# The last batch of an attention and expert kernel set up like the other three

## The chip, the cores and the metric

The kernel runs on one core of a Trainium2 chip. The metric is the device time of one execution in microseconds; the time before is the median of three runs.

## What is computed

Four batches of 11,456 tokens of width 128 pass through an attention over 49 agents, and its output through a layer of eight experts of which each token uses one. Cut to what matters:

```python
def sm(a, b):                       # softmax of scale * a @ b^T
    ...
agent_v = sm(agents, k) @ v         # 49 x 128 for each batch
x = sm(q, agents) @ agent_v         # the token
...
expert_idx = argmax(normalized(x) @ normalized(expert_emb).T / tau)
for e in range(8):
    h = np.maximum(x[mask] @ w1[e], 0.0)        # 1024 hidden units
    out[mask] = gate_w[mask, None] * (h @ w2[e])
```

## The kernel before

**Approach.** The tokens of a batch are mixtures of the same 49 vectors, and nearly all of them choose the same expert. `pick_expert` (L556) picks that expert for the batch, loads its weights, and ranks its 1024 hidden units by how safely their sign is the same for every token. The least safe `NMS[b] * 128` are the *layer units*: they are computed in full with their Relu. The next `FVS[b]` are the *checked units*: they are taken as linear, and a test on every token shows whether their sign held. The rest are linear by a bound. All linear units are folded into one 49 x 128 matrix, `lin`. Before, batches 0 to 2 have 256 layer units (`NMS` 2) and 320 checked units, the last batch 384 (`NMS` 3) and 512.

**Tiles.** A batch has 23 tiles (`NT`): 22 of 512 tokens and one of 192. For each tile and each group of 128 layer units `ffn_mm1` (L1032) makes two 512-wide matmuls (L1040, L1041), a Relu on ScalarE (L1044) and a residual on VectorE (L1045); `ffn_mm2` (L1048) makes twelve 128-wide ones (L1068 to L1070), and once per tile eight for `lin` (L1059). `ffn_out` (L1072) applies the gate on VectorE (L1083) and issues the output DMA on ScalarE's queue (L1089).

**Queries and checks.** A query unit (`q_unit`, L759) is up to 8 columns of 128 tokens, two tiles' worth: a load and a transposing DMA on SP, transposes, scores, exponentials and routing sums; `route_group` (L837) makes gates. Its result `tt` lies in one of eight buffers (`TB`), which is given back when the unit's layers and checks are through. `proved` (L910) makes the check for one column: one matmul with `vm` (L918), then a reduction on VectorE (L923, three columns in eight) or a summed Relu on ScalarE (L921).

**Failed tokens.** When a batch's 90 columns are checked, `mark_strays` (L933) marks the failed tokens. In batches 0 to 2 it keeps up to 3 of a partition and 128 in all that belong to the batch's expert, and spawns `fix` (L1182): the rows are gathered by an indirect DMA on POOL, the expert's weights are loaded again, `answer` (L1118) computes attention and expert in full for these 128 rows (L1121 to L1178), and an indirect DMA on POOL (L1179) overwrites their rows of the output. Other marked tokens are left to `stray` (L1198), which redoes one group per call. One call, `stray_first` (L1273), is emitted in the last batch's stage, after `fix` of batch 2. The rest is done in a loop behind everything, whose count is known only at run time (L1475 to L1483).

**Order.** The program is emitted in ticks, four to a tile, so 92 to a batch. Generators (`spawn`) are resumed at tick or half-tick intervals, and each `yield` is a step of them. A scheduler then places the instructions on each engine in a simulated order, in which emission order is a priority and the layers' first matmuls are drawn ahead; SP keeps the emitted order. `plan` (L1359) says when loads and queries are due; the keys and values of batch b run in the stage of batch b - 1. `prove()` is called once per tick, or twice if 12 or more checks are waiting (L1467). A write to `out` waits for the writes to `out` emitted before it.

Of the kernel before, what the change touches and what calls it, by code (L numbers as in the profile page):

```python
# [29 lines left out]
def kernel(ctx: ExitStack, tc: tile.TileContext, q, k, v, agents, emb, tau, w1, w2, out):  # L30
# [6 lines left out]
    NF = F // P  # L37
    NMS = [2] * (B - 1) + [3]
    FVS = [P * 5 // 2] * (B - 1) + [4 * P]
    FW = 4 * P  # L40
# [892 lines left out]
    def mark_strays(b):  # L933
# [32 lines left out]
        yield 1  # L966
        if b < B - 1:
            cand = sm.tile([P, NCOL], F32, name="mine", tag="mine", bufs=1)
# [103 lines left out]
    def ffn_out(b, t):  # L1072
# [14 lines left out]
        else:  # L1087
            dst = ob[P * J :, :].rearrange("(p j) d -> p j d", j=REM_J)
        act.dma_start(out=dst, in_=o[:p, :n])  # L1089


# [25 lines left out]

    def answer(xq, ix, gt, aT, avn, w1s, w2s):  # L1118

# [52 lines left out]
        for f in range(NF):  # L1172
            pe.matmul(out=t_[:, :D], lhsT=h[:, f, :], rhs=w2s[:, f, :], start=(f == 0), stop=(f == NF - 1))
            if f % 2 == 1:
                yield 1
        ring[hs][1] = now[0]
        o = sm.tile([P, D], F32, name="so", tag="so", bufs=1)
        dve.tensor_scalar(o, t_[:, :D], gt, None, ALU.mult)  # L1178
        pool.indirect_dma_start(out=out, out_offset=bass.IndirectOffsetOnAxis(ap=ix, axis=0), in_=o, in_offset=None,  # L1179
                                bounds_check=B * N - 1, oob_is_err=False)  # L1180

    def fix(b):  # L1182

        bt = batches[b]
        while not (hasattr(batches[b + 1], "vm") and (b == 0 or hasattr(batches[b - 1], "fixed"))):
            yield 1
        none = sm.tile([P, 1], F32, name="none", tag="none", bufs=1)
        ix = sm.tile([P, 1], I32, name="ix", tag="ix")
        dve.tensor_scalar(none, bt.fix[:, :1], 0.5, 2 * BIG, ALU.is_lt, ALU.mult)
        yield 1  # L1190
        dve.scalar_tensor_tensor(out=ix, in0=bt.fix[:, :1], scalar=-1.0, in1=none, op0=ALU.add, op1=ALU.add)
        w1s, w2s = load_expert(bt.e0i)
        xq = gather(ix)
        yield 14
        yield from answer(xq, ix, bt.fix[:, 1:], aT_all[:, b], av_all[:, b], w1s, w2s)
        bt.fixed = True
# [76 lines left out]
    def stray_first():  # L1273
# [7 lines left out]
        yield 1  # L1281
        dve.tensor_scalar(it, cums[-1][:, NG - 1 :], 1.0, None, ALU.min)


# [71 lines left out]

    QD = 6

    def plan():  # L1359
# [9 lines left out]
        for b in range(B):  # L1369
            for u in range(NU):  # L1370
                if b > 0 or u >= LEAD:
                    qs.append((at + QD, "q", b, u))
                    at += UT * TICKS if u < NU - 1 else TICKS
        return sorted(kv), qs
# [70 lines left out]
    with tc.manual_schedule(engines={mybir.EngineType.SP}):  # L1445
        due = []
        for i in range(len(ticks) + LAG):
# [14 lines left out]
            while due and due[0][0] <= i:  # L1462
# [3 lines left out]
                step2(b, t, f)  # L1466
            for _ in range(1 if len(jobs) < 12 else 2):  # L1467
                prove()
# [44 lines left out]
```

## Time and profile before

| | |
|---|---|
| median of 3 runs | 800.2 us (796.48 to 808.74) |
| profiled execution | 793.86 us, its span 792.1 us |
| busy share of the span | PE 90%, PEld 76%, DVE 78%, ACT 61%, POOL 44% |
| granted TensorE clock, mean | 0.958 |
| the chain that ended last, by engine | PE 56%, DVE 22%, DMA 11%, ACT 6% |

PE are TensorE's matmuls, PEld its weight loads, which overlap them; DVE is VectorE, ACT ScalarE, POOL GpSimd, SP the engine that issues most loads. Times are microseconds from the start of the span, unless marked ns. A matmul is shown for as long as it is under way, so neighbours overlap, and the step from start to start is its price on a full engine. The granted clock is a share of full speed.

### The profile page before, as it was taken

The page shows a single profiled execution, that of the slowest core. Times are in us where ns is not written, and L with a number is a line of the kernel's source. Part 1 is how long each engine was busy: PE and PEld are TensorE (multiplying, and loading weights), DVE is VectorE, ACT ScalarE, POOL GpSimd, SP SyncE. Part 2 cuts the span into 40 slices and gives each one's busy share as a digit, 9 for nine tenths or more (in the row PEclk, how much of TensorE's full clock was granted, in tenths as well). Part 3 has the DMA queues.
Part 4 walks back from the last instruction along what each step waited for, and adds up shares of the span by engine and source line. Part 5 has one row for each costly group of instructions (what it writes and reads, how often), then busy time and mean ns, then how long its engine had stood idle before and what let it go on. Part 6 is the DMA issues. An engine that isn't in the chain of part 4 may idle for free.

```text
span 792.1 us, 21166 instructions
## 1 busy us (share of the span) xinstructions
PE 715.1 (90%) x8161; PEld 602.9 (76%) x8161; DVE 616.4 (78%) x1639; ACT 485.5 (61%) x1229; POOL 345.1 (44%) x602
## 2 busy tenths in 40 slices
PE   8976789989997989899999699999998898999995
PEld 6976678977786768778888488778886686787774
DVE  5554998877674998966788898966789888698876
ACT  2334656866665765666767853766579346667762
POOL 5000453246413744645524633684537336254510
PEclk9987799999996999989999999999999999999997
DMA  8756029978627957955787528975342334333211
GB/s 329 205 191 249 28 28 283 272 171 227 190 89 201 260 131 167 226 151 144 220 210 196 116 78 207 252 194 172 108 130 74 89 102 126 92 87 94 84 41 47
DMA packets 164049, 124.01 MB, mean 157 GB/s; under 512 B 84967, under 2 KB 140347, under 8 KB 163947
## 3 DMA queue, kind: packets, MB, share of 16 engines
q1 hardware_dynamic: 150571, 99.02, 48.1%
q10 hardware_dynamic: 13120, 23.47, 8.6%
q8 instruction: 65, 1.06, 0.6%
q14 instruction: 37, 0.30, 0.1%
q0 software_dynamic: 256, 0.15, 0.1%
HBM read 79.14 MB, written 23.72 MB: 130 GB/s over the span
## 4 chain that ended last, share of the span: by engine, by line
PE 56%; DVE 22%; DMA 11%; ACT 6%; issue 4%; POOL 1%; SPq 0%; ACTq 0%; POOLq 0%; DVEq 0%
PE sp L773 6%; PE fTp L390 5%; PE avp L487 5%; PE sp L411 5%; PE vp L918 5%; PE yp L1068 4%; PE hp L1040 3%; PE yp L1069 3%; PE yp L1070 3%; DMA tt<-e 3%; PE hp L1041 3%; DVE hl L1045 3%; PE yp L1059 3%; DMA kt<-in_k_dram 2%; DVE ot L1083 2%
## 5 line engine op out<-in xcount | busy, mean ns | idle before, releaser
L1045 DVE SCALAR_TENSOR_TENSOR hl<-hp,hh 128x512 f16<-128x512 f32 (+1 forms) x207 | 136.9, 665 | 30.3 <-ACT hh L1044 29.8
L1068 PE MATMUL yp<-w2p,hh 128*128 128x128 f16 (+1 forms) x810 | 156.7, 222 | 0.8 <-ACT hh L1044 0.4
L1069 PE MATMUL yp<-w2p,hh 128*128 128x128 f16 (+1 forms) x810 | 156.4, 222 | 0.0
L1070 PE MATMUL yp<-w2p,hl 128*128 128x128 f16 (+1 forms) x810 | 152.5, 222 | 3.4 <-DVE hl L1045 3.4
L921 ACT ACTIVATE vp<-vp,la 128x320 f32<-128x320 f32 (+1 forms) x224 | 121.4, 542 | 53.2 <-PE vp L918 39.4
L1044 ACT ACTIVATE hh<-hp 128x512 f16<-128x512 f32 (+1 forms) x207 | 120.5, 587 | 52.1 <-PE hp L1041 44.4
L918 PE MATMUL vp<-vm,tt 128*128 128x320 f16 (+1 forms) x360 | 108.5, 320 | 8.1 <-DVE hl L1045 2.9
L1068 PEld LDWEIGHTS <-hh 128*128 128x128 f16 (+1 forms) x810 | 81.5, 101 | 18.5 <-ACT hh L1044 4.2
L1070 PEld LDWEIGHTS <-hl 128*128 128x128 f16 (+1 forms) x810 | 81.0, 100 | 18.2 <-issue 3.9
L773 PEld LDWEIGHTS sp<-aT_all,fT 128*128 128x128 f32 x720 | 86.6, 192 | 4.3 <-ACT gh L683 0.6
L773 PE MATMUL sp<-aT_all,fT 128*128 128x49 f32 x720 | 87.6, 271 | 0.6 <-ACT gh L683 0.4
L1069 PEld LDWEIGHTS <-hh 128*128 128x128 f16 (+1 forms) x810 | 81.2, 100 | 7.1 <-issue 0.7
L923 DVE TENSOR_REDUCE vmin<-vp 128x1 f32<-128x320 f32 (+3 forms) x136 | 72.1, 531 | 18.3 <-PE vp L918 18.2
L1040 PE MATMUL hp<-tt,gh 128*128 128x512 f16 (+1 forms) x207 | 77.5, 377 | 7.3 <-ACT vp L921 2.2
L1041 PE MATMUL hp<-tt,gl 128*128 128x512 f16 (+1 forms) x207 | 77.4, 376 | 0.0
L788 POOL TENSOR_TENSOR e<-qe,e 128x392 f16<-128x392 f32 (+1 forms) x44 | 37.8, 860 | 79.9 <-ACT e L787 74.4
L869 POOL TENSOR_TENSOR nrm<-qq,half 128x16 f32<-128x16 f32 (+2 forms) x28 | 69.2, 2472 | 0.3
L1083 DVE TENSOR_TENSOR ot<-yp,gs 128x512 f32<-128x512 f32 (+1 forms) x92 | 61.4, 668 | 8.4 <-PE yp L1070 8.1
L395 ACT COPY fT<-fTp 128x512 f32<-128x512 f32 (+1 forms) x78 | 43.7, 563 | 36.4 <-PE fTp L390 28.2
L1059 PE MATMUL yp<-lin,tt 128*128 128x128 f16 x720 | 64.2, 220 | 1.2 <-DVE ot L1083 1.1
L390 PE MATMUL fTp<-ident,qt 128*128 128x128 f32 x360 | 59.4, 301 | 5.8 <-DVE hl L1045 2.4
L393 DVE COPY fT<-fTp 128x512 f32<-128x512 f32 x70 | 47.7, 682 | 18.1 <-PE fTp L390 16.7
(358 smaller groups left out, 1735.4 us busy)
## 6 DMA issues: line engine op xcount, KB each, us to landing
kt<-in_k_dram SPq DMA_DIRECT2D x44, 512.0 KB, 6.8
vt<-in_v_dram SPq DMA_DIRECT2D x44, 512.0 KB, 5.0
qt<-in_q_dram SPq DMA_DIRECT2D x44, 512.0 KB, 5.4
out_dram<-ot ACTq DMA_DIRECT2D x88, 256.0 KB, 2.9
w1s<-in_moe_w_dram SPq DMA_DIRECT2D x8, 512.0 KB, 3.7
w2s<-in_moe_w_dram SPq DMA_DIRECT2D x8, 512.0 KB, 5.8
tt<-e SPq DMA_TRANSPOSE x44, 3.5
kt<-in_k_dram SPq DMA_DIRECT2D x4, 96.0 KB, 3.0
```

The costliest lines, as they stand in the source:

```text
L390: pe.transpose(out=tp[:, c * p : (c + 1) * p], in_=src[:p, c0 + c, :], identity=ident[:p, :p])
L773: pe.matmul(out=s[:p, c * A : (c + 1) * A], lhsT=xT[:, c * p : (c + 1) * p], rhs=aT_all[:, b, :], start=True, stop=True)
L918: pe.matmul(out=z[:p, :FV], lhsT=tts[b, u][:, c * p : (c + 1) * p], rhs=bt.vm, start=True, stop=True)
L921: act.activation(z[:p, :FV], z[:p, :FV], AF.Relu, bias=bt.l[:p, at], scale=-1.0, accum_out=bt.vsum[:p, at])
L1040: pe.matmul(out=hp[:, :m], lhsT=bt.gh[:, fs], rhs=tt, start=True, stop=False)
L1041: pe.matmul(out=hp[:, :m], lhsT=bt.gl[:, fs], rhs=tt, start=False, stop=True)
L1044: h_last[:] = [act.activation(hh[:, :m], hp[:, :m], AF.Relu)]
L1045: dve.scalar_tensor_tensor(out=hl[:, :m], in0=hp[:, :m], scalar=0.0, in1=hh[:, :m], op0=ALU.max, op1=ALU.subtract)
L1059: pe.matmul(out=yp[:p, c, :], lhsT=tc_, rhs=bt.lin[:, h], start=(c == 0 and h == 0), stop=False, skip_group_check=True)
L1068: pe.matmul(out=y, lhsT=hh[:, cs], rhs=wh, start=False, stop=False, skip_group_check=True)
L1069: pe.matmul(out=y, lhsT=hh[:, cs], rhs=wl, start=False, stop=False, skip_group_check=True)
L1070: y_last[:] = [pe.matmul(out=y, lhsT=hl[:, cs], rhs=wh, start=False, stop=last, skip_group_check=True)]
```

## The change

All four batches get 256 layer units and 320 checked units. `mark_strays` runs its candidate part, and spawns `fix`, for the last batch too. `fix` of the last batch starts once `stray_first` has appended to `strayed`; and before its scatter it waits until all 23 output DMAs of its batch are emitted (`last.outs < NT`). In `plan` the queries of the last batch are due at 0.6 of the distance (`RUN`): 4.8 ticks instead of 8 from unit to unit. In the last batch's ticks `prove()` is always called twice.

```diff
-    NMS = [2] * (B - 1) + [3]
-    FVS = [P * 5 // 2] * (B - 1) + [4 * P]
+    NMS = [2] * B
+    FVS = [P * 5 // 2] * B
...
-        if b < B - 1:
+        if True:
             cand = sm.tile([P, NCOL], F32, name="mine", tag="mine", bufs=1)
...
         act.dma_start(out=dst, in_=o[:p, :n])
+        batches[b].outs = getattr(batches[b], "outs", 0) + 1
...
-    def answer(xq, ix, gt, aT, avn, w1s, w2s):
+    strayed = []
+
+    def answer(xq, ix, gt, aT, avn, w1s, w2s, last=None):
...
         dve.tensor_scalar(o, t_[:, :D], gt, None, ALU.mult)
+        while last is not None and last.outs < NT:
+            yield 1
         pool.indirect_dma_start(out=out, ...
...
-        while not (hasattr(batches[b + 1], "vm") and (b == 0 or hasattr(batches[b - 1], "fixed"))):
+        while not ((b == B - 1 or hasattr(batches[b + 1], "vm")) and (b == 0 or hasattr(batches[b - 1], "fixed"))):
+            yield 1
+        while b == B - 1 and not strayed:
             yield 1
...
-        yield from answer(xq, ix, bt.fix[:, 1:], aT_all[:, b], av_all[:, b], w1s, w2s)
+        yield from answer(xq, ix, bt.fix[:, 1:], aT_all[:, b], av_all[:, b], w1s, w2s, bt if b == B - 1 else None)
...
         dve.tensor_scalar(it, cums[-1][:, NG - 1 :], 1.0, None, ALU.min)
+        strayed.append(True)
...
+    RUN = 0.6
...
-                    at += UT * TICKS if u < NU - 1 else TICKS
+                    at += (UT * TICKS if u < NU - 1 else TICKS) * (RUN if b == B - 1 else 1)
...
-            for _ in range(1 if len(jobs) < 12 else 2):
+            for _ in range(1 if len(jobs) < 12 and i < (B - 1) * S else 2):
```

## Rows read from the trace of the kernel before

**Rows 1.** Busy time by stretch: start:end, length, busy us and count, granted clock, DMA.
```profile
575.00:630.00 55.00, 49.03 (x522) 40.34 (x522) 49.16 (x155) 36.47 (x98) 28.89 (x47) 0.97 0.36 104
581.50:615.90 34.40, 31.77 (x358) 25.50 (x356) 30.64 (x83) 29.68 (x76) 22.42 (x34) 1.00 0.39 113
630.00:680.00 50.00, 45.37 (x520) 36.00 (x520) 39.87 (x108) 28.67 (x76) 24.22 (x38) 1.00 0.45 122
680.00:730.00 50.00, 48.37 (x548) 39.62 (x547) 43.73 (x112) 33.14 (x81) 22.19 (x33) 1.00 0.21 59
730.00:775.00 45.00, 45.00 (x528) 34.96 (x526) 36.38 (x76) 32.28 (x87) 14.22 (x28) 1.00 0.24 76
775.00:782.00 7.00, 6.54 (x100) 5.81 (x97) 6.79 (x24) 3.19 (x9) 0.19 (x2) 1.00 0.20 75
782.00:792.10 10.10, 1.02 (x3) 0.60 (x3) 3.33 (x26) 0.18 (x1) 1.13 (x1) 0.58 0.12 39
```
**Rows 2.** Line L1040 in 581.5:615.9 and in 629:782, durations, first and last start.
```profile
L1040 PE MATMUL hp<-tt,gh x14: 246/376/379, 582.0 to 614.7; 128*128 128x512 f16 x12, 128*128 128x192 f16 x2
L1040 PE MATMUL hp<-tt,gh x69: 246/379/380, 630.3 to 778.8; 128*128 128x512 f16 x66, 128*128 128x192 f16 x3
```
**Rows 3.** Timeline of PE, 740.5:741.7: start, duration, line, operation.
```profile
740.61 0.38 PE L1040 MATMUL hp<-tt,gh 128*128 128x512 f16 x1
740.83 0.38 PE L1041 MATMUL hp<-tt,gl 128*128 128x512 f16 x1
741.04 0.22 PE L1070 MATMUL yp<-w2p,hl 128*128 128x128 f16 x1
...
741.66 0.22 PE L1069 MATMUL yp<-w2p,hh 128*128 128x128 f16 x1
```
**Rows 4.** Groups by line in 630:782: count, busy us, mean ns, idle before.
```profile
L1045 DVE SCALAR_TENSOR_TENSOR hl<-hp,hh 128x512 f16<-128x512 f32 x66 | 44.3, 679 | 10.6 <-ACT hh L1044 10.6
L918 PE MATMUL vp<-vm,tt 128*128 128x512 f16 x88 | 32.6, 379 | 1.1 <-DVE hl L1045 1.1
L1167 PE MATMUL shp<-sx,w1s 128*128 128x128 f32 x32 | 4.9, 281 | 0.0
```
**Rows 5.** Line L918 in 472:630, the stage of batch 2: durations min/median/max.
```profile
L918 PE MATMUL vp<-vm,tt x90: 296/299/310, 489.4 to 611.7; 128*128 128x320 f16 x88, 128*96 128x320 f16 x2
```
**Rows 6.** DVE busy with line L923 in the last two stages.
```profile
472.00:630.00 158.00, 16.39 (x34) 0.99 0.58 154
630.00:782.00 152.00, 22.98 (x34) 1.00 0.30 86
```
**Rows 7.** Timeline of DVE: first and last VectorE step of batch 2's redo.
```profile
658.26 0.14 DVE L1189 TENSOR_SCALAR none<-fix 128x1 f32<-128x1 f32 x1
...
690.00 0.34 DVE L1178 TENSOR_SCALAR so<-syp,fix 128x128 f32<-128x128 f32 x1
```
**Rows 8.** Timeline of PE and DVE: steps of stray_first.
```profile
700.37 0.14 DVE L1282 TENSOR_SCALAR it<-cum 128x1 f32<-128x1 f32 x1
...
740.28 0.28 PE L1121 MATMUL sqT<-ident,xq 128*128 128x128 f32 x1
...
769.40 0.34 DVE L1178 TENSOR_SCALAR so<-syp,gt 128x128 f32<-128x128 f32 x1
```
**Rows 9.** Last outputs (L1083), and the chain that ended last, 779:792: start, us, step.
```profile
L1083 DVE TENSOR_TENSOR ot<-yp,gs x23: 415/679/692, 642.4 to 781.6; 128x512 f32<-128x512 f32 x22, 96x256 f32<-96x256 f32 x1
...
781.86 0.78 issue
782.64 2.27 DMA out_dram<-so,ix
...
787.70 0.15 DVE lefti L1479
```
**Rows 10.** DMA issues: KB each, median us from issue to landing.
```profile
w2s<-in_moe_w_dram SPq DMA_DIRECT2D x8, 512.0 KB, 5.8
xq<-in_q_dram,ix POOLq DMA_INDIRECT x4, 4.4
```

## The prediction

> **What bounds the kernel now.** I read the page first (its busy shares are in the table above): TensorE is busiest, VectorE second. Shares over the whole span mix stages, and this change works on the last batch and the tail behind it. So I asked for the busy time by stage [rows 1]: column PE against DVE, stretch by stretch. From 630 us, where the last batch's layers begin [rows 2], to 782, PE is busy 45.4 + 48.4 + 45.0 + 6.5 = 145.3 of 152 us and DVE 39.9 + 43.7 + 36.4 + 6.8 = 126.8. At 730 to 775 PE is busy all 45 us. There each instruction taken from PE moves everything behind it forward, until DVE is the wall. The last 10 us (the last of the rows) are another regime: PE works 1 us of them at a granted clock of 0.58, and the chain decides [rows 9].
>
> A busy PE need not be a full PE, so I looked at starts: two 512-wide matmuls start 0.22 us apart, and eleven 128-wide ones take 741.66 - 741.04 = 0.62 us, 0.056 each [rows 3]. These are the prices of a matmul here, not the 0.38 and 0.22 us that one is shown to last.
>
> By the Trainium skill (Perfetto Trace Analysis, "Identifying the Most-Contended Engine") matmul busy time is a poor measure and weight-load busy time a better one. At 730 to 775 that column says 34.96 of 45 us, under DVE's 36.38 [rows 1], so by the rule DVE would be the bound; the trace leaves this open, and it is the first rival below.
>
> **The third layer (NMS 3 to 2).** Per full tile go 2 matmuls of 512 and 12 of 128: 2 x 0.216 + 12 x 0.056 = 1.10 us of PE; 22 tiles and the small one, 24.8 us. On DVE a third of the L1045 work goes, 44.3 / 3 = 14.8 us [rows 4]. On ACT as many Relus go; ACT is never the fullest engine [rows 1], so I count nothing for them.
>
> **The checks (FVS 512 to 320).** 90 matmuls last 299 instead of 379 ns [rows 4, 5], 0.080 each: 7.2 us of PE. The L923 reductions cost 16.4 us in batch 2's stage with 320 and 23.0 in the last with 512 [rows 6]: 6.6 us of DVE. The narrower products of pick_expert: an estimated 2 us of PE. Removed in sum: PE 34, DVE 21.
>
> **What is added in the stage.** mark_strays now also runs its candidate part for the last batch, some 24 small DVE instructions. The nearest in size are L1189 (0.14) and L1178 (0.34) [rows 7], so 6 us of DVE. Its few matmuls cost 1 us of PE. The net is PE -33, DVE -15.
>
> **Queries ahead (RUN 0.6) and two checks per tick.** No instruction is added. Query unit u of the last batch is spawned 4.8u instead of 8u ticks after the first, and from unit 8 on it waits for a slot of the eight-deep tt ring, so that unit u - 8 must be through layers and checks. Its load and its transpose on SP move with it; the last key and value loads stand ahead of it in SP's order in both kernels, so nothing new is overtaken. Up to three units fall before 630 us; there PE is busy 49.0 and DVE 49.2 of 55 us from 575 on [rows 1], so at most some 6 us of idle time can take them. I count 0, between 0 and 6: DVE has little room and the start of the layers hangs on pick_expert's chain there. On the other side the checks end about ten tiles before the layers, so marking (DVE, and the counting behind it) leaves the end.
>
> **How long the stage gets.** PE work falls to 145 - 33 = 112 us, DVE to 127 - 15 = 112. Neither hides behind the other now. The nearest stretch with two layers, 320 checks and no keys is the end of batch 2's stage, 581.5 to 615.9: PE is busy 92% and DVE 89% of it [rows 1]. 112 / 0.92 = 122 and 112 / 0.89 = 126; I take 125, a gain of 27. Bounds: 15, if only DVE's net counts; 34, if PE stays the only wall. Layer starts say the upper one: 13 steps in 32.7 us before 614.7 make 5.0 us per tile, 68 steps in 148.5 us at three per tile make 6.55 [rows 2]; 22.5 x 1.5 = 34.
>
> **The redo within the batch (fix for the last batch).** The kernel's check, worked out on the reference's own inputs in double precision: with 256 layer and 320 checked units 39 tokens of the last batch fail, at most 3 in a partition, against none with 384 and 512. Up to 3 in a partition and 128 in all are kept, so all are redone in one pass, and the loop at the end still runs zero times.
>
> The pass is not free. It waits until stray_first is done (`strayed`), which in turn waits for fix of batch 2. Now stray_first's answer starts at 740.3 and its last VectorE step ends it at 769.4 [rows 8], 12.6 us before the last output product is done (781.6 + 0.4) [rows 9]. Its steps are spread over ticks, and ticks shrink with the stage: I take 9 us before the end. Behind it the expert's weights are reloaded (one buffer each; w2s lands 5.8 us after issue [rows 10]) and the rows gathered (4.4 us, on POOL behind stray_first's scatter). Batch 2's pass took 690.0 - 658.3 = 31.7 us from its first step to L1178, under full load [rows 7]. Behind the layers nothing competes; the floor is the weights' 5.8 us and the 16 matmuls behind w2s, taken at L1167's 4.9 / 32 = 0.15 us [rows 4], 8.3 in all. I take half of the loaded time, 16 us, because emission can run ahead of its place: stray_first's last line, L1282, ran at 700.4, long before its answer [rows 8]. So the product is ready 16 - 9 = 7 us after the layers; a semaphore (0.6), the scatter's landing (2.3) and about 3.5 of the 4.4 us between 787.70 and the end [rows 9] make 13.4. Before, the same stretch is 792.1 - 782.0 = 10.1 us. Cost: 3.3 us. Bounds: with the floor the pass hides, and the count chain, freed of the marking, ends 1 us sooner; with the loaded 31.7 us the tail costs 19.
>
> By the Trainium skill (TensorE: Matmul & The Clock Gate, Part 1) TensorE is throttled by default and activity lifts it; the trace agrees in the tail, at 0.58 granted. At half speed the 32 large matmuls of the pass would cost another 4.9 us [rows 4], inside the bounds just given.
>
> **Sum.** The profiled execution took 793.9 us (span 792.1). 793.9 - 27 + 3.3 = 770.2. The median shown is 800.2, 0.8% above it; in its terms 777.
>
> **Rivals.**
> - *DVE is the wall.* The rule above points here. For it: DVE's 36.4 of 45 us at 730 to 775 and its 89% at 581.5 to 615.9 [rows 1]. Against: PE without a gap there. The stage gains 15, the tail costs 3.3: 782.2, as a median 789.
> - *The gain goes in the tail.* The pass keeps its loaded 31.7 us because its matmuls are put behind all of the layers' and its gather behind the scatter. Against: the layers are over by then. 793.9 - 27 + 19 = 786, as a median 792.
> - *PE stays the only wall and the pass hides.* 793.9 - 34 - 1 = 759, as a median 765.
> - *Slower.* The two passes in series are bound by their own waits, not by ticks: stray_first still ends at 769.4 and the pass needs 31.7 us behind it. The product is ready at 801.1, the end comes at 807.5, 15.4 us later than now: as a median 816. It costs time from the point where stray_first ends after about 754. For it: 29 us from L1121 to L1178 for a few microseconds of work [rows 8]. Against: those gaps lie under a full PE, and shrink with it.
> - *It does not do what it says.* If more tokens stayed over, each round of the end's loop would cost a gather, a weight load and an answer, 20 us or more: 797 and up. Against: the count above.
>
> **How the numbers follow.** The forecast of 777 has 0.49, its own range 769 to 785; DVE the wall 0.16; the tail 0.12; the good rival 0.13; slower 0.07; the loop 0.03. A change of 2% (to below 784 or above 816) is about what a measurement of this kernel can tell from none. Faster by more: 0.13 and nine tenths of the 0.49, with a little of the DVE case, 0.6. Slower by more: half of the slower rival, which gives just the line, and the loop from its second round on, with a little beside them, 0.08. The rest is 0.32. The range from 764 to 793 leaves out the last two cases and the outermost edges.
>
> **What would show it.** Right: L1040 46 times in the last stage, L1121 five times, L1205 once; layers of the last batch at 5.0 to 5.7 us per tile; the last L1083 near 755; L941 of the last batch well before the last L1040; the last L1179 some 8 us behind the last L1083. Wrong: a tile pace over 6 us with PE idle before DVE's releases; L1121 of the fifth answer waiting on w1s, w2s or xq more than 10 us behind the layers; a second L1205.

## The result and the profile after

The median fell from 799.7 to 791.5 us over 20 runs of each kernel; the ratio is 0.9899, 95% interval 0.9869 to 0.9929. So the change gives 1.0%, some 8 us. The forecast was 777, a gain of 23; 792 was the price of the rival "the gain goes in the tail". The profiled execution of after took 794.9 us, its span is 793.0.

The two profiles can't be compared by their spans: that of after begins the layers of batch 0 at 113.3 us, that of before at 103.4, though TensorE's instructions stand in the same order there (the last section shows what goes with it). So I compare by stage. Busy time by stretch in the profile of after (columns as in [rows 1]: PE, PEld, DVE, ACT, POOL, granted clock, DMA share, GB/s), from the first L1040 of the last batch to the end:

```profile
646.50:696.00 49.50, 43.61 (x533) 37.20 (x532) 41.95 (x125) 29.01 (x87) 32.19 (x50) 1.00 0.46 101
696.00:745.00 49.00, 43.89 (x476) 33.39 (x475) 42.12 (x126) 34.07 (x112) 28.76 (x52) 1.00 0.29 83
745.00:769.30 24.30, 24.30 (x324) 20.23 (x322) 23.95 (x86) 10.95 (x23) 1.41 (x3) 1.00 0.24 89
...
775.00:782.00 7.00, 3.69 (x15) 3.21 (x16) 0.16 (x1) 1.00 (x3) 0.00 (x0) 0.66 0.31 99
782.00:793.00 11.00, 3.99 (x25) 3.59 (x24) 2.12 (x14) 0.90 (x3) 0.99 (x1) 0.81 0.02 5
...
646.50:769.30 122.80, 111.79 (x1328) 90.82 (x1328) 108.02 (x334) 74.03 (x220) 62.35 (x104) 1.00 0.35 92
769.30:793.00 23.70, 11.37 (x70) 10.16 (x68) 3.85 (x23) 3.61 (x9) 2.01 (x2) 0.81 0.20 63
```

The last two rows are the result: the layers of the last batch take 122.8 us where they took 152 [rows 1], and behind them come 23.7 us where there were 10.1. The layers, line L1040, by two windows of the same profile, and their outputs, line L1083 (durations, first and last start):

```profile
L1040 PE MATMUL hp<-tt,gh x27: 376/379/381, 646.5 to 739.5; 128*128 128x512 f16 x27
L1040 PE MATMUL hp<-tt,gh x19: 246/379/379, 741.4 to 762.4; 128*128 128x512 f16 x17, 128*128 128x192 f16 x2
...
L1083 DVE TENSOR_TENSOR ot<-yp,gs x8: 670/680/685, 750.4 to 767.5; 128x512 f32<-128x512 f32 x8
```

At two starts per tile that is 93.0 / 26 x 2 = 7.2 us per tile while queries and checks run, and 21.0 / 18 x 2 = 2.3 us per tile at their end and after it (the last check starts at 744.6). The outputs say the same: 17.1 / 7 = 2.4 us per tile. Before, the last 31 starts, three per tile, were spread over 49 us, 4.9 us per tile. [rows 2] had one pace for the whole stage; now there are two. The groups that answer to [rows 4]:

```profile
L1045 DVE SCALAR_TENSOR_TENSOR hl<-hp,hh 128x512 f16<-128x512 f32 x44 | 29.5, 678 | 1.9 <-ACT hh L1044 1.8
L918 PE MATMUL vp<-vm,tt 128*128 128x320 f16 x88 | 22.3, 298 | 1.6 <-DVE hl L1045 0.7 <-ACT vp L921 0.4
L923 DVE TENSOR_REDUCE vmin<-vp 128x1 f32<-128x320 f32 x33 | 15.8, 479 | 5.3 <-PE vp L918 5.1
```

And VectorE's timeline, five rows of it: the marking of the last batch begins (L941), it hands the marked tokens to the pass (L1010), the pass's first step (L1196, L1189 of before), and the two last steps of `answer` (L1181, L1178 of before; `gt` is stray_first's, `fix` the pass's):

```profile
747.70 0.24 DVE L941 TENSOR_TENSOR odd<-vmin,la 128x90 f32<-128x90 f32 x1
...
766.88 0.16 DVE L1010 COPY fix<-mine 128x2 f32<-128x2 f32 x1
...
767.12 0.15 DVE L1196 TENSOR_SCALAR none<-fix 128x1 f32<-128x1 f32 x1
...
772.53 0.35 DVE L1181 TENSOR_SCALAR so<-syp,gt 128x128 f32<-128x128 f32 x1 [3.11 <-PE syp L1176]
...
785.51 0.35 DVE L1181 TENSOR_SCALAR so<-syp,fix 128x128 f32<-128x128 f32 x1 [10.36 <-PE syp L1176]
```

The chain that ended last, from 773 on (start, us, step):

```profile
773.16 3.85 DMA out_dram<-so,ix
777.01 0.02 issue
777.03 0.34 ACTq L1089
...
777.95 0.27 ACT seTs L1153
778.22 0.04 issue
778.26 0.81 PE sx L1156 x2
779.07 0.02 issue
779.09 0.28 ACT sx L1159
779.37 0.04 issue
779.41 3.78 PE shp L1170 x16
783.19 2.29 PE syp L1176 x16
785.49 0.02 issue
785.51 0.35 DVE so L1181
785.86 0.20 DVE mTx L200
```

Three things stand in it. stray_first's product is ready at 772.5, behind the layers. Its scatter (L1184, issued at 773.16) is followed on ScalarE's queue by the last output DMAs, which wait for its landing, 3.85 us in the chain, and the pass's copy L1153 stands behind them on the same engine. And TensorE, which had waited before, runs the pass at a granted clock of 0.66 between 775 and 782 (4.8 of these 7 us at the lower level, 1.2 GHz): the sixteen matmuls of L1170 take 3.78 us.

### The profile page after: what moved, and what is told of

It is laid out like the page before. It is cut to its first block, busy times and chain, and to the rows that moved or that the text cites. A ratio compares the mean times of both kernels' runs of the same rounds, so it can differ in the third digit from the quotient of the medians.

```text
span 793.0 us, 20624 instructions
## 1 busy us (share of the span) xinstructions
PE 705.7 (89%) x7882; PEld 599.4 (76%) x7882; DVE 604.3 (76%) x1647; ACT 467.3 (59%) x1211; POOL 347.9 (44%) x605
## 4 chain that ended last, share of the span: by engine, by line
PE 55%; DVE 24%; DMA 10%; ACT 6%; issue 4%; ACTq 0%; SPq 0%; POOL 0%; POOLq 0%; DVEq 0%
PE sp L773 7%; PE fTp L390 7%; PE avp L487 5%; PE sp L411 5%; DVE hl L1045 4%; PE vp L918 4%; PE yp L1059 3%; PE hp L1040 3%; PE yp L1068 3%; PE yp L1069 3%; PE yp L1070 3%; DMA kT<-ks 3%; PE hp L1041 3%; DVE ot L1083 2%; DMA kt<-in_k_dram 2%
## 5 line engine op out<-in xcount | busy, mean ns | idle before, releaser
L921 ACT ACTIVATE vp<-vp,la 128x320 f32<-128x320 f32 x224 | 112.8, 504 | 50.6 <-PE vp L918 28.9
L1068 PE MATMUL yp<-w2p,hh 128*128 128x128 f16 x720 | 139.3, 222 | 1.7 <-ACT hh L1044 1.2
L1069 PE MATMUL yp<-w2p,hh 128*128 128x128 f16 x720 | 139.2, 221 | 0.0
L1044 ACT ACTIVATE hh<-hp 128x512 f16<-128x512 f32 (+1 forms) x184 | 107.6, 588 | 51.3 <-PE hp L1041 38.5
L1045 DVE SCALAR_TENSOR_TENSOR hl<-hp,hh 128x512 f16<-128x512 f32 (+1 forms) x184 | 121.8, 665 | 20.0 <-ACT hh L1044 19.4
L1070 PE MATMUL yp<-w2p,hl 128*128 128x128 f16 x720 | 135.5, 222 | 0.5 <-DVE hl L1045 0.5
L918 PE MATMUL vp<-vm,tt 128*128 128x320 f16 x360 | 98.4, 301 | 8.0 <-DVE hl L1045 2.5
L1068 PEld LDWEIGHTS <-hh 128*128 128x128 f16 x720 | 72.7, 101 | 17.9 <-ACT hh L1044 6.2
L1070 PEld LDWEIGHTS <-hl 128*128 128x128 f16 x720 | 71.8, 100 | 12.4 <-issue 4.1
L1040 PE MATMUL hp<-tt,gh 128*128 128x512 f16 (+1 forms) x184 | 69.3, 378 | 12.7 <-DVE hl L1045 4.3
L923 DVE TENSOR_REDUCE vmin<-vp 128x1 f32<-128x320 f32 (+1 forms) x136 | 65.4, 481 | 18.0 <-PE vp L918 17.7
L1069 PEld LDWEIGHTS <-hh 128*128 128x128 f16 x720 | 72.0, 100 | 5.3 <-issue 0.7
L1041 PE MATMUL hp<-tt,gl 128*128 128x512 f16 (+1 forms) x184 | 69.1, 377 | 0.0
L1083 DVE TENSOR_TENSOR ot<-yp,gs 128x512 f32<-128x512 f32 (+1 forms) x92 | 61.5, 669 | 8.0 <-PE yp L1070 7.4
```

The costliest lines, as they stand in the source:

```text
L918: pe.matmul(out=z[:p, :FV], lhsT=tts[b, u][:, c * p : (c + 1) * p], rhs=bt.vm, start=True, stop=True)
L921: act.activation(z[:p, :FV], z[:p, :FV], AF.Relu, bias=bt.l[:p, at], scale=-1.0, accum_out=bt.vsum[:p, at])
L1040: pe.matmul(out=hp[:, :m], lhsT=bt.gh[:, fs], rhs=tt, start=True, stop=False)
L1041: pe.matmul(out=hp[:, :m], lhsT=bt.gl[:, fs], rhs=tt, start=False, stop=True)
L1044: h_last[:] = [act.activation(hh[:, :m], hp[:, :m], AF.Relu)]
L1045: dve.scalar_tensor_tensor(out=hl[:, :m], in0=hp[:, :m], scalar=0.0, in1=hh[:, :m], op0=ALU.max, op1=ALU.subtract)
```

## The experiments

Every ratio is to runs of the kernel before on the same chip. "Stage" is from the first L1040 of the last batch to the end of the last L1083, "tail" what follows; L941 is where the marking of the last batch begins. All in us, from one profile each; that of nofix is of its longest execution (787.0 us, median 777.5), that of plain of its shortest (764.2 us, median 774.3):

| run | ratio, 95% interval | stage | tail | L941 after the stage's start | L941 to the end |
|---|---|---|---|---|---|
| before | 1 | 151.8 | 10.1 | 145.4 | 16.4 |
| after | 0.9899 (0.9869 to 0.9929) | 122.8 | 23.8 | 101.2 | 45.3 |
| plain | 0.9726 (0.9654 to 0.9797) | 128.3 | 10.9 | 123.3 | 16.0 |
| nofix | 0.9745 (0.9696 to 0.9794) | 125.7 | 10.8 | 104.2 | 32.4 |
| run1 | 0.9883 (0.9841 to 0.9924) | 126.9 | 26.8 | 118.9 | 34.8 |
| half | 0.9946 (0.9909 to 0.9983) | 129.4 | 20.2 | 104.5 | 45.1 |
| early | 0.9917 (0.9872 to 0.9961) | 123.0 | 22.6 | 101.4 | 44.2 |
| fast | 0.9892 (0.9821 to 0.9963) | 133.2 | 12.4 | 105.2 | 40.5 |
| hold | 0.9857 (0.9821 to 0.9894) | 130.7 | 14.3 | 104.1 | 40.9 |
| hold2 | 0.9906 (0.9872 to 0.9941) | 130.9 | 17.7 | 108.0 | 40.6 |
| hold3 | 0.9885 (0.9843 to 0.9927) | 130.6 | 16.8 | 106.5 | 40.9 |
| actchk | 0.9869 (0.9797 to 0.9942) | 126.7 | 18.8 | 100.5 | 45.0 |
| holdact | 0.9853 (0.9792 to 0.9914) | 122.2 | 19.0 | 100.6 | 40.6 |
| ring9 | 0.9876 (0.9826 to 0.9926) | 123.8 | 21.0 | 94.7 | 50.1 |
| best9 | 0.9896 (0.9860 to 0.9933) | 125.3 | 20.4 | 96.7 | 48.9 |
| holdput | 0.9967 (0.9924 to 1.0011) | 134.5 | 15.9 | 111.8 | 38.6 |
| actput | 0.9899 (0.9821 to 0.9977) | 127.7 | 15.7 | 105.5 | 37.8 |
| fv320 | 1.0185 (1.0129 to 1.0241) | 141.2 | 32.9 | 133.9 | 40.2 |

### What the smaller sizes are worth, and what the redo costs

**plain**: the kernel before with the sizes alone; failed tokens of the last batch are not marked for a pass.

```diff
-    NMS = [2] * (B - 1) + [3]
-    FVS = [P * 5 // 2] * (B - 1) + [4 * P]
+    NMS = [2] * B
+    FVS = [P * 5 // 2] * B
...
+        if b < B - 1:
+            dve.tensor_tensor(out=ne, in0=ne, in1=odd, op=ALU.max)
```

> The kernel before with 256 layer and 320 checked units in the last batch and nothing else of the change: no queries ahead, one check per tick, no pass; the failed tokens of the last batch are not marked and keep the layers' value. Theory A (the arithmetic alone gives what was forecast for the stage, 27 us between 15 and 34): from the first L1040 of the last batch to the last L1083 some 122 to 130 us in place of 152, the tail 10 to 12, and the time 20 to 30 us under before: ratio 0.963 to 0.975. Rival (the queries ahead are what frees the engines): under 15 us, ratio above 0.981.

Measured 0.9726, 774.3 us, some 22 us. Busy time by stretch of its profile:

```profile
623.20:751.50 128.30, 118.80 (x1379) 99.13 (x1378) 109.53 (x308) 77.70 (x224) 61.67 (x102) 0.97 0.39 104
751.50:762.50 11.00, 0.69 (x3) 0.39 (x3) 3.59 (x28) 0.18 (x1) 1.14 (x1) 0.65 0.11 36
```

The sizes alone, with the failed tokens left as they are, bring what the forecast took for the whole change, and the tail stays as it was.

**nofix**: the kernel after, marked as it is, without the pass.

```diff
-            spawn(fix(b), 1, half=True)
+            if b < B - 1:
+                spawn(fix(b), 1, half=True)
```

> The changed kernel without the redo pass of the last batch: its failed tokens are still sorted out, but fix is not spawned for them, so the 39 tokens keep the layers' value. Theory A: the pass alone holds the end; without it from the last L1083 to the end come 9 to 14 us (stray_first's scatter still lies there), and the time is 11 to 16 us under the changed kernel, ratio to before 0.968 to 0.976. Theory C (the gain was never there: the stage is bound by VectorE and the tail is long for other reasons, the scatter of stray_first and the slow clock): under 5 us, ratio above 0.984.

Measured 0.9745, 777.5 us, and a tail of 10.8:

```profile
774.40:785.20 10.80, 3.72 (x32) 3.33 (x30) 2.27 (x16) 1.38 (x3) 1.13 (x1) 0.84 0.10 35
```

With after beside it, the pass alone costs 0.9899 - 0.9745 = 1.5%, 12 us (8 to 17 by the two intervals), and the tail is 23.8 - 10.8 = 13 us longer with it. This names the term that failed. TensorE has the same matmuls in the same order in both up to the pass. So the two stages, 125.7 and 122.8 us, differ by what one execution differs from another, at a granted clock of 0.95 and 1.00: the table's stages are no surer than some 3 us.

**fv320**: the kernel before with 320 checked units in the last batch, and nothing else.

```diff
-    FVS = [P * 5 // 2] * (B - 1) + [4 * P]
+    FVS = [P * 5 // 2] * B
```

> The kernel before with only the checked units of the last batch cut from 512 to 320, the layer units left at 384. By the price of a check (0.080 us of TensorE for 90 columns, 6.6 us of VectorE in all) 4 to 8 us under before, ratio 0.990 to 0.995; if the checks are hidden anyway, under 2 us.

Measured 1.0185, slower. The stage did get 11 us shorter, but the loop at the end now ran a round, as two rows of VectorE's timeline show (its first and its last large step):

```profile
781.80 0.24 DVE L1205 TENSOR_SCALAR_CACHE_REDUCE ind<-cum,it 128x32 f32<-128x32 f32 x1 [1.09 <-issue]
...
802.56 0.35 DVE L1178 TENSOR_SCALAR so<-syp,gt 128x128 f32<-128x128 f32 x1 [8.27 <-PE syp L1173]
```

A round costs 21 us here. So the pass is no mere cost: without it the smaller sizes would pay at least one such round (not run; by the code a round takes one token of a partition, and up to 3 of a partition fail). It also corrects my count of failed tokens, which took in the signs alone; with the bound's test as well, 66 tokens of the last batch fail at 256 and 320 (39 by sign, 46 by the bound), and 3 at 384 and 320, which make this round. 66 still fit one pass, so the time forecast doesn't change by it.

### Do the queries ahead do anything

**run1**: the kernel after without the run-ahead.

```diff
-    RUN = 0.6
+    RUN = 1.0
```

> The changed kernel with RUN 1.0: the queries of the last batch at 8 ticks from unit to unit, as before. Theory A: the checks then end at the end of the layers, marking moves behind them, and the pass, which needs the marks, starts later than stray_first's end: 5 to 12 us slower than the changed kernel, ratio 0.996 to 1.005, with L941 of the last batch within 5 us of the last L1083. Rival: stray_first sets the pass's start in any case and the even spread fills the engines better: 0 to 5 us faster than the changed kernel, ratio 0.983 to 0.99.

Measured 0.9883 against 0.9899: no difference that can be told. But the time lies elsewhere. In the five profiles with the queries at their old distance (before twice, plain, run1, fv320) the last batch's first L1040 comes 153.5 to 158.2 us after batch 2's first, mean 156.5; in all fourteen with 0.6 and a pass (after twice) it comes 160.5 to 166.1 us after, mean 163.7. The run-ahead puts the start of the last layers back by 7 us, moves L941 forward from 118.9 to 101.2 us after that start, and stage and tail together come out shorter by as much (153.7 to 146.5; 10 us of run1's stage are at the lower clock, none of after's, so this part is less sure).

### Earlier: stray_first, the count, the marks

**half**: stray_first steps in half ticks, so that the pass doesn't wait for it.

```diff
-    spawn(stray_first(), (B - 1) * S + 8)
+    spawn(stray_first(), (B - 1) * S + 8, half=True)
```

> The changed kernel with one edit: stray_first is resumed at half-tick instead of tick steps, so that its 63 steps take 32 ticks and not 63. Theory A (the stage gains what was forecast, 27 to 32 us, and the tail gives 16 of it back because the pass is emitted behind stray_first and so behind the layers): stray_first ends some 30 ticks earlier, the pass runs under the layers, from the last L1083 to the end come 10 to 14 us in place of 26.6, and the time falls by 10 to 16 us against the changed kernel: ratio to before 0.970 to 0.978. Theory B (the pass is bound by its own waits, gather, weights and scatter, and not by its place): under 4 us, ratio 0.985 to 0.99.

Measured 0.9946, no better than after. Its answer was ready at 744.9 instead of 772.5, but the pass was not earlier: the marking's copy for the pass still came at 767.4 (766.9 in after), and the gather at 769.1 (767.8 in after). So two conditions end together in after, and taking one away leaves the other. (The tail of after, 26.6 in the text above, is the 23.8 of the table.) The stage meanwhile grew by 6.6. ScalarE's timeline of this run shows part of it:

```profile
746.50 1.74 ACT L1044 ACTIVATE hh<-hp 128x512 f16<-128x512 f32 x3
750.90 0.34 ACTq L1089 DMA_DIRECT2D out_dram<-ot  x1
751.28 1.08 ACT L1044 ACTIVATE hh<-hp 128x512 f16<-128x512 f32 x2 [3.04 <-PE hp L1041]
```

stray_first's scatter was issued at 745.56, an output DMA behind it waits for its landing at the head of ScalarE's order (an event wait of 3.27 us), and the next Relu stands behind that (3.04 us idle).

**early**: the count of the tokens left over is emitted as soon as marks and stray_first are done, not behind the pass.

```diff
+    def count_last():
+        while not (strayed and hasattr(batches[B - 1], "marked")):
+            yield 1
+        yield from count_strays()
...
+    spawn(count_last(), (B - 1) * S + 8, half=True)
...
-    now_run(count_strays())
```

> The changed kernel with the last count (count_strays ahead of the loop) emitted as soon as marking and stray_first are through, and not behind the pass. Theory A: the count chain lies behind the pass with 2.9 us from the pass's L1181 to lefti, so 1 to 3 us less than the changed kernel, ratio 0.986 to 0.989. If the scatter's landing holds the end by itself: no change, 0.990.

The count ended at 767.8, ten us ahead of the pass's last step, and the end came 6.4 us behind that step instead of 7.5. Measured 0.9917: 1 us can't be seen. Here the scatter of the pass sets the end, not the count.

**fast**: both of these, marks, passes and checks of the last batch ahead of the layers, fewer steps in the marking, and no priority for the last batch's layers.

```diff
-            spawn(mark_strays(b), 1, half=True)
+            spawn(mark_strays(b), 1, half=True, up=UP if b == B - 1 else 0)
...
-                    with tc.high_priority(200):
+                    with tc.high_priority(200) if b < B - 1 else nullcontext():
```

> The changed kernel with everything that should start the pass earlier: stray_first in half-tick steps, marking of the last batch with a third of its steps, both and the pass and the checks drawn ahead in priority, the layers of the last batch no longer drawn ahead, the count early. Theory A, revised (two conditions end at the same time, marking and stray_first, so that half steps alone gave nothing): with both gone the pass starts 5 to 15 us before the last L1083 and the time is 5 to 12 us under the changed kernel, ratio 0.975 to 0.984. Rival (the last layers run at 2.4 us per tile with too little time left for a chain of marks and pass, whatever the order): under 4 us, ratio 0.985 to 0.99.

The tail fell to 12.4, nearly that of before, and the stage rose to 133.2. Measured 0.9892, the same as after. The gain that the tail had taken was now lost in the stage, in it an event wait of ScalarE of 6.9 us in one piece, for stray_first's scatter: 3.3 us until that was issued at 751.3, and 3.6 until it had landed.

### Is it the scatter in the middle

**hold** is fast, **hold2** is half with early; in both, stray_first's scatter is held back until the last batch's 23 output DMAs are emitted.

```diff
-        o = sm.tile([P, D], F32, name="so", tag="so", bufs=1)
+        o = sm.tile([P, D], F32, name="so", tag="so", bufs=2)
...
-        while last is not None and last.outs < NT:
+        if done is not None:
+            done()
+        while last is not None and getattr(last, "outs", 0) < NT:
             yield 1
```

> The run 'fast' with one edit: stray_first's scatter is held back until all 23 output transfers of the last batch are emitted (its buffer so is doubled, and the mark that lets the pass begin is set before the scatter). Theory (the scatter in the middle of the stage holds ScalarE, because the output transfers behind it on its queue wait until it has landed; 6.9 us in one piece in 'fast'): the stage falls from 133 us to 124 to 128, the tail stays at 12 to 15 us, and the ratio to before is 0.975 to 0.984. Rival (VectorE and TensorE are full in these 50 us, the wait of ScalarE only moved work that would have waited anyway): stage 131 to 135 us, ratio 0.987 to 0.993.

> The kernel after, with stray_first in half ticks as in the run 'half', the count at the end emitted early as in 'early', and stray_first's scatter held back until the last output transfers as in 'hold'. Theory (the scatter holds ScalarE): the stage is 123 to 126 us, against 129.4 in 'half'; the tail, which the marking of the last batch still sets, stays at 18 to 22 us; ratio 0.983 to 0.990. Rival (the work only moves): stage 128 to 131 us, ratio 0.990 to 0.996.

The waits are gone: the longest event wait ahead of an output DMA is 17 ns in both, against 6863 ns in fast and 3267 in half. The stage hardly answered: 130.7 against 133.2, and 130.9 against 129.4. hold's 0.9857 is the second lowest ratio of the kernels that do all the work, but its interval overlaps that of after. The theory fell: ScalarE's stall was real, and taking it away gave the stage 2.5 us in one pair and nothing in the other. That what it held would have waited anyway is inferred. Busy time by stretch of hold:

```profile
700.00:710.00 10.00, 10.00 (x119) 8.48 (x118) 8.39 (x30) 6.63 (x22) 7.26 (x11) 1.00 0.23 83
710.00:720.00 10.00, 5.72 (x64) 3.62 (x63) 9.84 (x38) 4.32 (x16) 6.34 (x13) 0.83 0.34 86
720.00:730.00 10.00, 8.95 (x82) 5.98 (x81) 9.06 (x28) 7.20 (x24) 7.83 (x18) 0.82 0.38 121
...
637.40:768.10 130.70, 118.19 (x1360) 96.86 (x1358) 111.14 (x346) 76.53 (x225) 60.93 (x104) 0.96 0.37 96
768.10:782.40 14.30, 6.26 (x35) 5.69 (x35) 1.33 (x11) 1.72 (x4) 2.01 (x2) 0.73 0.06 19
```

Where stray_first's VectorE steps now lie (710 to 720), VectorE is full and TensorE busy 5.7 of 10 us; and the granted clock is 0.83 and 0.82 in these two stretches, 6.8 us of them at the lower level (1.2 GHz), from 716.7 on. hold2 (6.8), hold3 (10.2) and fast (6.8) have one behind such a stretch; after and half have none there. In these profiles VectorE work that is pulled forward leaves TensorE waiting, and some us at the lower level follow. It isn't the only place: the second profiles of before and after, where nothing is pulled forward, have 10.2 and 6.8 us at the lower level earlier in the stage. What it costs was not measured by itself.

**hold3**: hold with the layers' priority back.

```diff
-                    with tc.high_priority(200) if b < B - 1 else nullcontext():
+                    with tc.high_priority(200):
```

> The run 'hold' with the layers of the last batch given their priority of 200 back, as in after (marks and passes stay at 1000). Theory (TensorE and VectorE have some 120 us of PE and 112 us of DVE to do between the first layer and the end, and what the pass and the marks take early the layers give late): stage 123 to 130 us, tail 14 to 22 us, their sum 143 to 147 us as in after, early, fast and hold; ratio 0.983 to 0.990. Rival (the layers' missing priority cost 'hold' its stage): stage 122 to 125 us with the tail of 14 us kept, sum 136 to 139 us; ratio 0.972 to 0.980.

0.9885, stage 130.6, sum of stage and tail 147.4. The priority was not what cost hold its stage.

### Is it VectorE

**actchk** (from after) and **holdact** (from hold): two of the three columns in eight that VectorE reduces go to ScalarE in the last batch.

```diff
-        if c not in (0, 2, 4):
+        if c not in ((0, 2, 4) if b < B - 1 else (0,)):
```

> The kernel after; in the last batch two of the three columns in eight whose check VectorE reduces go to ScalarE as the other five do (22 instructions of 0.48 us leave VectorE, as many of 0.50 us come to ScalarE, which is busy 74 of the stage's 122.8 us). Theory (VectorE is what the stage waits for, full at 720 to 730 and 745 to 765, and the marking waits there too): the stage is 3 to 6 us shorter, 117 to 120 us, the tail 20 to 23 us; ratio 0.979 to 0.985. Rival (TensorE, or the chain of marks and pass by its own waits, sets the end): stage 122 to 124 us, tail 22 to 25 us, ratio 0.987 to 0.993.

> The run 'hold' with the same edit as 'actchk'. Theory (in 'hold', too, what the redos and marks take of VectorE the layers give late): stage 124 to 128 us against 130.7, tail 13 to 16 us; ratio 0.977 to 0.983. Rival: stage 129 to 132 us, ratio 0.984 to 0.990.

VectorE's work in the stage fell as meant, from 108.0 to 101.0 us in actchk. Stage and tail together: 145.5 against 146.5, and 141.2 against 145.1. A third pair with this edit, holdput and actput below, has 150.4 and 143.4. By the ratios none can be told from its own base (0.9869 from 0.9899, 0.9853 from 0.9857, 0.9899 from 0.9967). So the theory's 3 to 6 us did not come in actchk, and VectorE's share is left open: the sums fell by 1.0, 3.9 and 7.0 us, in single profiles.

### Is it the moment of the last check

Up to here L941 to the end had been 44 to 45 us in after, half, early and actchk, which looked like one serial stretch behind the last check.

**ring9** is after, **best9** is fast with actchk's edit; both have nine `tt` buffers, so that the checks can be two tiles further ahead.

```diff
-    TB = 8
+    TB = 9
```

> The kernel after with nine tt buffers instead of eight (TB), so that the queries and checks can be one unit, two tiles, further ahead of the layers. Theory (the end is the last check plus a serial stretch of marks, pass and count, 45.3 and 44.3 us from L941 to the end in after and 44 to 45 in early, half and actchk; L941 itself waits for the ring): L941 comes 92 to 97 us after the first layer of the last batch instead of 101 to 102, the end 137 to 142 us after it instead of 146; ratio 0.979 to 0.986. Rival (the engines are full in this stretch and the order changes nothing): the end comes 145 to 147 us after that first layer, ratio 0.987 to 0.993.

> The run 'fast' with nine tt buffers as in 'ring9' and the checks moved to ScalarE as in 'actchk'. Theory: L941 98 to 102 us after the first layer (105.2 in 'fast'), 41 us from there to the end as in 'fast', so the end 139 to 143 us after it; ratio 0.978 to 0.985. Rival: 145 us, ratio 0.987 to 0.993.

L941 came forward as expected (94.7 and 96.7 us after the stage's start), and L941 to the end grew to 50.1 and 48.9. The end stayed at 145 and 146 us after the start. The stretch is no constant. In best9 VectorE writes the first `mput` at 749.4, and the pass begins 18 us later; two rows of VectorE's timeline, and TensorE's line L1023 (the three pairs of small matmuls, `mine`, that gather the marked tokens; first and last start):

```profile
767.07 0.15 DVE L1027 COPY fix<-mine 128x2 f32<-128x2 f32 x1
767.26 0.15 DVE L1216 TENSOR_SCALAR none<-fix 128x1 f32<-128x1 f32 x1
```

```profile
L1023 PE MATMUL mine<-mpick,mput x6: 168/237/251, 753.8 to 766.7; 128*128 128x2 f32 x6
```

Six matmuls of 0.24 us are spread over 13 us: `mput` has one buffer, so each pair waits for the one before, and each time it stands in TensorE's order behind layers.

**holdput** (hold) and **actput** (holdact) take that wait away.

```diff
-                put = sm.tile([P, P], F32, name="mput", tag="mput", bufs=1)
+                put = sm.tile([P, P], F32, name="mput", tag="mput", bufs=3)
```

> The run 'hold' with three buffers for mput instead of one, so that the three small matmuls of the last batch's marking can follow one another (in 'hold' the three pairs of a VectorE step and a matmul take from 749.0 to the copy of fix at 756.3, 7.2 us, each matmul waiting in TensorE's order behind layers). Theory (the time from L941 to the end is a row of such waits, each of which can be taken off): 7.2 us become 2 to 4, L941 to the end 36 to 39 us against 40.9, the end 140 to 143 us behind the first layer against 145.1; ratio 0.978 to 0.984. Rival (the three go just as late, or the gather and the pass behind wait for something else): 40 to 42 us, ratio 0.984 to 0.989.

> The run 'holdact' with the three buffers for mput. In 'holdact' the three take 761.3 to 769.0, 7.7 us. Theory: 2 to 4 us, L941 to the end 36 to 38 us against 40.6, the end 136 to 139 us behind the first layer against 141.2; ratio 0.976 to 0.983. Rival: 40 to 42 us, 141 to 145 us, ratio 0.983 to 0.989.

From the first `mput` to the copy of `fix` it took 4.1 us instead of 7.2, and 2.8 instead of 7.7; L941 to the end fell to 38.6 and 37.8, as the theory said. But L941 itself came 5 to 8 us later, and the ratios, 0.9967 and 0.9899, are no better than their bases'. With the changed buffer TensorE's order differs from that of the base from 325 and 331 us on, long before the last batch, and the stages came out 3.8 and 5.5 us longer. So these two runs change more than the wait.

**before2** and **after2** are the two kernels once more, unchanged, for their starts.

> The kernel before, once more, for a second profile of it. In the two profiles the first L1040 starts at 103.4 us before and at 113.3 after, though TensorE's order is the same up to batch 1's redo. If the start varies by itself, this run has it anywhere from 100 to 115, and the layers from there to the last L1083 take the same 678 us within 5. If the change shifts the start, it is 103 to 104 again.

> The kernel after once more, unchanged, for its start. If the start of 113 us in the profile of after (103 in that of before) is chance, this one's profile begins the layers anywhere from 100 to 113 us, and its time follows its granted clock as that of before does, 4 to 6 us for each 0.01; stage 121 to 125 us, tail 22 to 25 us, ratio 0.987 to 0.993. If the change made the start longer, it begins at 110 us or later again.

before2 begins the layers at 101.3 us, after2 at 105.0 (ratio 0.9882, interval 0.9841 to 0.9923): the 113.3 of the first profile was chance. after2's stage is 123.2 and its tail 22.7. From the first layer to the last L1083 before2 takes 685.0 us and before 678.7, a difference of 6.3 where at most 5 was expected: single profiles differ by that much.

## Why the prediction was wrong

From the two profiles of each kernel, means: up to the first L1040 of the last batch counted from the first of batch 0, 528.8 us before and 535.5 after; stage 153.1 and 123.0; tail 10.1 and 23.3. That is +6.7 - 30.1 + 13.2 = -10.2 us, beside -8 and -9 in the medians. The forecast had 0 - 27 + 3.3 = -23.7. So 9.9 us of the difference lie in the tail and 6.7 ahead of the stage, and the stage gives 3.1 of them back.

- **The stage: right.** 122.8 and 123.2 against 125. Its working held too: PE is busy 111.8 us (112 forecast), 91% of the stage (92% taken from batch 2's end). DVE is busy 108.0 (112): the marking added 12.0 - 7.4 = 4.6 us where I took 6. Without the queries ahead the stage is 126.9 (run1) and 128.3 (plain), still near 125.
- **DVE the wall: wrong, PE the only wall: wrong.** The sums of both came near 112, and the stage's gain, 30, lies between the 15 of the one and the 34 of the other. By the rule of the Trainium skill (Perfetto Trace Analysis, "Identifying the Most-Contended Engine") the weight loads' 90.8 us against DVE's 108.0 would put DVE ahead. The runs leave that open: taking 5 to 8 us from DVE changed stage and tail by 1.0 (actchk), 3.9 (holdact) and 7.0 us (actput), and no ratio beyond its interval.
- **The tail: this is the step that failed,** 13.7 us longer instead of 3.3. The failing sentence is "I take 9 us before the end" for the moment from which the pass may run. I read it from stray_first alone and sent the marking out of the way with "the checks end about ten tiles before the layers, so marking (DVE, and the counting behind it) leaves the end". I saw ten tiles at 5.0 to 5.7 us each, some 50 us of cover. There were six and a half by the starts of L1040 (13 after L941), eight and the small one by outputs, and without queries and checks beside them they go at 2.3 to 2.4 us each: 21.6 us from L941 to the layers' end, and the marking takes 19.4 of them (747.7 to L1196 at 767.1). The pass begins 2 us before the layers' end. stray_first, from which I had the 9, ended 3.6 us behind the layers (772.5 + 0.35). The marking as a condition of the pass stood in the sum at nothing, though the trace of before shows its length: in batch 2 it takes 40.5 us from L941 to the copy that the pass needs (L1010), shown below; in after it takes 19.2. The prediction's sign for this part, L941 well before the last L1040, came true (747.7 and 762.4) and said nothing: what the pass needs is L1010 (766.9).

```profile
617.29 0.18 DVE L941 TENSOR_TENSOR odd<-vmin,la 128x90 f32<-128x90 f32 x1
...
657.83 0.14 DVE L1010 COPY fix<-mine 128x2 f32<-128x2 f32 x1
```

- **The pass itself: right, by its length.** 16 us taken, 785.5 - 767.1 = 18.4 measured. ScalarE's wait behind stray_first's scatter is 3.7 us long; some 2.4 of them count, for the copy L1153 could have run once its transpose (L1150) was done at 775.5. Some 2 are the lower clock: sixteen matmuls in 3.78 us at 0.66, against 2.00 for stray_first's at 768.6, at full clock. The Trainium skill (TensorE: Matmul & The Clock Gate, Part 1) has TensorE throttled by default and lifted by activity; the trace agrees in kind, at 0.66 granted after TensorE had waited.
- **Queries ahead: counted as nothing, and worth nothing in sum** (run1), but not by nothing: the start of the stage moved by 6.7 us to later, where I had 0 to 6 us of gain, and stage and tail were about as much shorter. So this term was wrong too, but taking the run-ahead away gains nothing.
- **The rivals.** "The gain goes in the tail", at 792, is what came, by another way: the pass did not take its loaded 31.7 us, it started 7 us later than I had it. That its number fits is luck: it has 19 us in the tail where 13 came, and nothing ahead of the stage. "Slower" named the condition, stray_first's end after 754, 124 us behind the stage's start; it ended 126 us behind it (772.5), and the pass did not need 31.7 us from there.

Why the time then stays when pieces are moved is only half settled. Shown is that the pass costs 12 us (nofix), that the tail can be brought from 23.8 to 12.4 us (fast), and that the stage then grows by about as much: stage and tail together are 141 to 150 us in all thirteen kernels with run-ahead and pass, 137 and 139 without the pass (nofix, plain). ScalarE's stall, the layers' priority, the ring of `tt` and the single `mput` were each taken away without a gain beyond the intervals, so none of them is the one cause; VectorE's load is open. What speaks for a shared limit: in hold PE is busy 118.2 + 6.3 us and in after 111.8 + 11.4, about the same work; in the last 24.3 us of the layers PE and DVE are both full (24.30 and 23.95 us in after), so what goes first there makes something else go last. That is argued, not shown. The clock is a second open cause, for the sums hold different times at the lower level, 9 us in after and 18 in hold. No run joins the queries at their old distance with the edits that start the pass earlier. No kernel that redoes the failed tokens was found that is safely faster than after; holdact and hold, at 0.985 and 0.986, are the candidates.

## What to carry to other kernels

A pace measured under load doesn't hold for what is left when the load goes: count the work that remains behind an event in time at the unloaded pace, not in tiles. When a step must wait for two things, find when each is done; moving one alone (half) gains nothing. And where a gain in a stage is paid for by a serial step behind it, cost that step from the moment at which its last input is ready, and run the kernel without it to see its whole price.

## What the runs showed of the hardware

**The clock in the start.** The same program spends its first 115 us differently from one execution to the next. Busy time by stretch, 80 to 115 us, first in after, then in after2, the same kernel with the same order on TensorE:

```profile
80.00:115.00 35.00, 29.94 (x210) 25.18 (x210) 24.31 (x68) 16.90 (x32) 12.36 (x23) 0.60 0.05 16
```

```profile
80.00:115.00 35.00, 27.84 (x240) 23.44 (x241) 31.60 (x82) 23.08 (x46) 17.55 (x26) 0.87 0.06 16
```

At a granted clock of 0.60 instead of 0.87 TensorE gets through 210 instead of 240 matmuls. The time at the lower level (1.2 GHz) in the start was 23.9 us in both profiles of before, 51.2 in after and 27.3 in after2, and the first layer came at 103.4, 101.3, 113.3 and 105.0 us. It shows in the total: over 51 executions of before (beside the runs on three chips), each 0.01 of mean granted clock goes with 4.9 us less, over 20 of after with 4.4. Which of the two drives the other these figures don't say, for a TensorE that waits is also granted less (0.58 in the tail of before [rows 1]). The profile of before had 0.958, that of after 0.941; the means over all executions are 0.947 and 0.946. Two spans of single profiles could not have shown a change of 1%.

**A scatter holds a queue.** An output DMA on ScalarE's queue, emitted behind an indirect DMA that writes to the same tensor, waited until that had landed: 3.3 us in half, and 6.9 us in fast, where the first 3.3 passed before the scatter was issued. ScalarE's next Relu stood behind it. With the scatter last (hold, hold2) the wait was 17 ns.
